# The opening of a two-layer kernel: half means subtracted in one VectorE step, transposes evacuated two blocks at a time, and the second tile centred in halves

## The chip, the cores and the metric

The kernel runs on one core of a Trainium2 chip. The metric is the device time of one execution in microseconds (us).

## The reference

Two layers, each an attention over 8 positions 2 apart and a gated feed-forward part, on 2048 tokens of width 1024. Only the first lines matter here: the layer norm of the input and the projection to q.

```python
def _layernorm(x, axis=-1, eps=1e-5):
    m = jnp.mean(x, axis=axis, keepdims=True)
    v = jnp.var(x, axis=axis, keepdims=True)
    return (x - m) / jnp.sqrt(v + eps)
# ...
x = A_x                                              # [1, 2048, 1024] bf16
x = x + _A_ref(_layernorm(x, axis=-1), A_wqkv, A_wo) # begins with layernorm(x) @ wqkv
```

## The kernel before

The kernel lists its operations with an estimated duration each, places them on a modelled timeline, sorts them by the modelled start and emits them in that order. So a change of one estimate can change the order of instructions on a queue. "AQ" in the model is ScalarE's queue as an issuer of DMAs; the model treats it as an engine beside ScalarE, but line 257 of the kernel issues these DMAs with `nc.scalar.dma_start`, so they stand in one emitted order with ScalarE's own work.

The opening brings 512 tokens (four tiles of 128) and the q weights (eight rows of 256 KB, "row 0" to "row 7") in, and projects the first two tiles while the weights are still landing. The division by the standard deviation is done later, so tiles 0 and 1 need only their mean:

```python
def q_first():
    # x tile 0 in halves on both queues, x tile 1 on ScalarE's; rows 0-4, x tile 3, rows 5, 7 on SyncE's
    # ... cut ...
    dve(0.45, <sum of the left half of x tile 0>,  ..., [("xn", 2), ("part", 0)], -9)
    act(0.75, <sum of the right half of x tile 0>, ..., [("xn", 3), ("part", 1)], -9)
    dma(256, x_sb[2][:], xin[:, 2, :], [("part", 1)], ..., queue="AQ")
    dve(0.16, <mean = (part0 + part1) / D>, ..., [("mean", 0)], -9)
    act(1.15, <mean of x tile 1>, ..., [("xn", 3), ("mean", 1)], -9)
    rows[2](6, queue="AQ", after=[("mean", 1)])       # weight row 6: issued from ScalarE's queue
    for j in range(2):                                # tiles 0 and 1
        # tile 0 centred in halves, tile 1 in one piece (DVE); 8 transposes (PE);
        # first four blocks evacuated by DVE, last four by ACT
        # ... cut ...
    # tiles 2, 3: full layer norm on DVE, then transposes
    # ... cut ...
    for kk, j0, j1 in [(k, j, j + 1) for j in range(2) for k in range(3)] + [(k, 0, 2) for k in range(3, KT)]:
        # 8 (j1 - j0 = 1) or 8 wide matmuls of weight row kk
        # ... cut ...
    wslots[1] = q_weights(1, "s")                     # k weights: two loads of 1 MB, SyncE's queue
```

Of the kernel before, what the change touches and what calls it, by code (L numbers as in the profile page):

```python
# [9 lines left out]
ALU = mybir.AluOpType  # L10
ACTF = mybir.ActivationFunctionType
# [22 lines left out]
class Program:  # L34
# [5 lines left out]
    def add(self, eng, dur, emit, reads=(), writes=(), cls=2, lag=0.0, size=0, takes=(), gives=(), lane=0,  # L40
            table=None):
        op = Op(len(self.ops), eng, dur, emit, tuple(reads), tuple(writes), cls, lag, size, tuple(takes),
                tuple(gives), lane, table)
        for k in op.reads:
            if k in self.last_w:
                op.deps.add(self.last_w[k])
        for k in op.writes:
            if k in self.last_w:
                op.deps.add(self.last_w[k])
            op.deps.update(self.last_r.get(k, ()))  # L50
        op.deps.discard(op)
        for k in op.reads:
            self.last_r.setdefault(k, []).append(op)
        for k in op.writes:
            self.last_w[k] = op
            self.last_r[k] = []
        for a in op.takes + op.gives:
            a.users.append(op)
            a.left += 1
        self.ops.append(op)  # L60
        return op
# [95 lines left out]
def kernel(  # L157
# [11 lines left out]
    nc = tc.nc  # L169
    P = 128  # L170
    _, S, D = A_x.shape
    F = B_w1.shape[1]
    KT = D // P
# [8 lines left out]
    scale = float(Dh) ** -0.5  # L182
# [4 lines left out]
    xin = A_x[0].rearrange("(n p) d -> p n d", p=P)  # L187
# [12 lines left out]
    def alloc(name, shape, dt=BF16):  # L200
        return sb.tile(shape, dt, name=name)

    ident = alloc("ident", [P, P])
# [3 lines left out]
    x_sb = [alloc(f"x{n}", [P, D]) for n in range(S // P)]  # L207
    xnT = [alloc(f"xnT{i}", [P, KT, CH]) for i in range(2)]
    xn = [alloc(f"xn{i}", [P, D]) for i in range(4)]
# [23 lines left out]
    part = alloc("part", [P, 2], FP32)  # L233
    mean = alloc("mean", [P, 2], FP32)
# [5 lines left out]
    pr = Program()  # L240
# [7 lines left out]
    def dve(dur, emit, reads, writes, cls=2, **kw):  # L248
        return pr.add("DVE", dur, emit, reads, writes, cls, **kw)

    def act(dur, emit, reads, writes, cls=0, **kw):
        return pr.add("ACT", dur, emit, reads, writes, cls, **kw)

    def dma(kb, dst, src, reads, writes, cls=3, transpose=False, queue="SP"):
        def emit(op):
            if queue == "AQ":
                nc.scalar.dma_start(dst, src)
            elif transpose:
                nc.sync.dma_start_transpose(dst, src)
            else:  # L260
                nc.sync.dma_start(dst, src)
        return pr.add(queue, 0.45, emit, reads, writes, cls, size=kb * 1024)
# [20 lines left out]
    for i in range(NWARM):  # L283
        a = Acc()
# [66 lines left out]
    def evac(add, dur, emit, last_mm, reads, writes, a, cls=0, **kw):  # L351
        op = add(dur, emit, reads, writes, cls, gives=[a], **kw)
        op.deps.add(last_mm)
        return op
# [62 lines left out]
            q_tile(l, c, which, ws, b)  # L417
        stage_no[0] += 1

    def transposed(src, keys, dst, dkeys):  # L420
        for h, add, fn, dur in ((0, dve, nc.vector.tensor_copy, 0.42), (1, act, nc.scalar.copy, 0.59)):
            a = Acc()
            k0 = 4 * h

            def tr(op, a=a, k0=k0):
                pt = bank[a.bank][:].bitcast(BF16)
                for k in range(4):
                    nc.tensor.transpose(pt[:, k * P:(k + 1) * P], src[:, (k0 + k) * P:(k0 + k + 1) * P], ident[:])  # L428
            tro = pr.add("PE", 0.25, tr, [keys[h], "ident"], [], takes=[a], lag=0.17, lane=2)

            def emit(op, a=a, k0=k0, fn=fn):
                pt = bank[a.bank][:].bitcast(BF16)
                fn(dst[:, k0:k0 + 4, :], pt[:, 0:4 * P].rearrange("p (k t) -> p k t", k=4))  # L433
            evac(add, dur, emit, tro, [], dkeys[k0:k0 + 4], a, cls=-9)

    def q_first():
        for hh in range(2):
            dma(128, x_sb[0][:, hh * 512:(hh + 1) * 512], xin[:, 0, hh * 512:(hh + 1) * 512], [], [("x", 0, hh)], 0,
                queue="AQ" if hh else "SP")
# [3 lines left out]
        for kk in range(5):  # L443
# [3 lines left out]
        rows[2](7)  # L447
        b, q, stats, root, apply = ln(0, first=True)
        ce = hT[:, 8:16, :]
        dve(0.45, lambda _: nc.vector.tensor_scalar(xn[2][:, 0:512], x_sb[0][:, 0:512], 0.0, 0.0, op0=ALU.add,  # L450
                                                    op1=ALU.add, accum_out=part[:, 0:1]),
            [("x", 0, 0)], [("xn", 2), ("part", 0)], -9)
        act(0.75, lambda _: nc.scalar.activation(xn[3][:, 0:512], x_sb[0][:, 512:1024], ACTF.Copy,  # L453
                                                 accum_out=part[:, 1:2]), [("x", 0, 1)], [("xn", 3), ("part", 1)], -9)
        dma(256, x_sb[2][:], xin[:, 2, :], [("part", 1)], [("x", 2, 0), ("x", 2, 1)], 0, queue="AQ")
        dve(0.16, lambda _: nc.vector.tensor_scalar(mean[:, 0:1], part[:, 0:1], part[:, 1:2], 1.0 / D, op0=ALU.add,  # L456
                                                    op1=ALU.mult), [("part", 0), ("part", 1)], [("mean", 0)], -9)
        act(1.15, lambda _: nc.scalar.activation(xn[3][:], x_sb[1][:], ACTF.Copy, scale=1.0 / D,
                                                 accum_out=mean[:, 1:2]), [("x", 1, 0), ("x", 1, 1)],
            [("xn", 3), ("mean", 1)], -9)  # L460
        rows[2](6, queue="AQ", after=[("mean", 1)])
        for j in range(2):
            for h0, h1 in ((0, 1), (1, 2)) if j == 0 else ((0, 2),):
                dve(0.5 if j else 0.32, lambda _, j=j, c0=512 * h0, c1=512 * h1: nc.vector.tensor_scalar(  # L464
                    xn[j][:, c0:c1], x_sb[j][:, c0:c1], mean[:, j:j + 1], None, op0=ALU.subtract),
                    [("x", j, 0), ("x", j, 1), ("mean", j)], [("xn", j)] + [("xn", j, h) for h in range(h0, h1)], -9)
            transposed(xn[j], [("xn", j, h) for h in range(2)], ce[:, :, j * P:(j + 1) * P],
                       [("ce", j, k) for k in range(KT)])
        for j in range(2, TPC):
            stats(j, [("ce", 1, 0)])  # L470
            root(j, j + 1)
            apply(j)
            transposed(xn[j], [("xn", j)] * 2, xnT[b][:, :, j * P:(j + 1) * P],
                       [("xnT", b, j, k // 4) for k in range(KT)])
        for j in range(2):
            act(1.25, lambda _, j=j: nc.scalar.activation(sgt[j][:].rearrange("p a b -> p (a b)"), x_sb[j][:],
                                                          ACTF.Square, bias=mean[:, j:j + 1], scale=-1.0,
                                                          accum_out=part[:, j:j + 1]),
# [3 lines left out]
                                                         scale=1.0 / D),  # L482
# [21 lines left out]
        for kk, j0, j1 in [(k, j, j + 1) for j in range(2) for k in range(3)] + [(k, 0, 2) for k in range(3, KT)]:  # L504
            lk = [q_lhs(wslots[0], kk, m) for m in range(KT)]

            def emit(op, kk=kk, j0=j0, j1=j1, lk=lk, pa=pa):
                for m in range(KT):
                    t0 = (m % 2) * 2 * P
                    nc.tensor.matmul(bank[pa[m // 2].bank][:, t0 + j0 * P:t0 + j1 * P], lhsT=lk[m][0],  # L510
                                     rhs=ce[:, kk, j0 * P:j1 * P], start=(kk == 0 and m % 2 == 0 and j0 == 0),
                                     stop=(kk == KT - 1), skip_group_check=True)
            op = pr.add("PE", 8 * (j1 - j0) * 0.0545, emit,
                        [lk[0][1]] + [("ce", j, kk) for j in range(j0, j1)], [], takes=pa, lag=0.17)
# [193 lines left out]
    def attend(l, c):  # L708
        for r in range(R):
            t_stage(l, c * R + r)  # L710

    q_first()
    attend(0, 0)
    for c in range(1, NCH):
# [47 lines left out]
```

## Time and profile before

| | before |
|---|---|
| time, median of the first 3 runs | 1614.96 us (1614.81 to 1615.19) |
| span of the profiled execution | 1613.4 us |
| TensorE busy | 99% |
| TensorE's gaps after its warm-up | 0.20 us and 0.18 us, both before 6.6 us |
| first full-width projection matmul | 21.89 us |

The page of the kernel before, its line of busy time, and the chain of work that ended last:

```profile
PE 1601.8 (99%) x7463; PEld 763.1 (47%) x7610; DVE 1121.7 (70%) x1904; ACT 330.7 (20%) x527; POOL 5.3 (0%) x28
...
PE 99%; issue 1%; DMA 0%; DVE 0%; ACT 0%
PE bank L347 98%; PE bank L510 0%; PE bank L524 0%; DMA x<-in_A_x_dram 0%; PE bank L428 0%; ACT xn L453 0%; DVE hT L433 0%; DVE xn L464 0%; DVE x L689 0%; DVE mean L456 0%; ACT L281 0%
```

TensorE works without a gap above 0.06 us from 6.52 us to the end.

The timeline of the opening before. Columns: start, length, engine, line, operation, output and input, count, and the idle time of the engine before it with what ended it.

```profile
4.52 0.19 ACT L453 ACTIVATION_READ_ACCUMULATOR xn<-x 128x1 f32 x1
4.74 0.21 DVE L456 TENSOR_SCALAR mean<-part 128x1 f32<-128x1 f32 x1 [0.29 <-ACT xn L453]
4.99 0.62 DVE L464 TENSOR_SCALAR xn<-x,mean 128x512 bf16<-128x512 bf16 x2
...
5.40 0.94 PE L428 MATMUL bank<-ident,xn 128*128 128x128 bf16 x8 [0.20 <-DVE xn L464]
5.42 0.33 ACTq L257 DMA_DIRECT2D slot<-in_A_wqkv_dram  x1
6.04 0.42 DVE L433 COPY hT<-bank 128x512 bf16<-128x512 bf16 x1 [0.44 <-PE bank L428]
...
6.52 1.05 PE L510 MATMUL bank<-hT,slot 128*128 128x128 bf16 x16 [0.18 <-DVE hT L433]
...
7.41 0.61 PE L428 MATMUL bank<-ident,xn 128*128 128x128 bf16 x8
```

Line 456 is the addition that the change removes, line 464 the centring, 428 the transposes, 433 the evacuation, 510 the first weight matmuls. The line at 5.42 is the issue of weight row 6. Later on, the same timeline filtered to TensorE shows an unbroken row of matmuls through row 6's (due at 12.27) and the start of the full-width matmuls:

```profile
10.74 2.56 PE L510 MATMUL bank<-hT,slot 128*128 128x256 bf16 x22
13.14 1.06 PE L428 MATMUL bank<-ident,xn 128*128 128x128 bf16 x16
14.04 1.04 PE L510 MATMUL bank<-hT,slot 128*128 128x256 bf16 x8
...
21.89 2.32 PE L347 MATMUL bank<-xnT,slot 128*128 128x512 bf16 x9
```

### The profile page before, as it was taken

How to read it: one execution, taken by the hardware profiler on the slowest of the kernel's cores; microseconds unless marked ns; L12 is line 12 of the kernel's file. 1: busy time of each engine (PE TensorE's matmuls, PEld its weight loads, DVE VectorE, ACT ScalarE, POOL GpSimd, SP SyncE). 2: the span in 40 equal slices, each digit the busy share in tenths (PEclk: the TensorE clock that was granted, in tenths of full speed). 3: DMA queues.
4: the chain of work that ended last, by engine and by line, in shares of the span. 5: the costliest groups of instructions: out<-in, count | busy, mean ns of one | idle time of the engine just before them, and what ended most of it. 6: DMA issues, size and time to landing. Idle time of an engine off the chain costs nothing.

```text
span 1613.4 us, 19079 instructions
## 1 busy us (share of the span) xinstructions
PE 1601.8 (99%) x7463; PEld 763.1 (47%) x7610; DVE 1121.7 (70%) x1904; ACT 330.7 (20%) x527; POOL 5.3 (0%) x28
## 2 busy tenths in 40 slices
PE   9999999999999999999999999999999999999999
PEld 7555544444444444444444444444444444444444
DVE  5898888889889888888898729884288832211211
ACT  5423322021211222113211032110321101101110
POOL 1000000000000000000000000000000000000000
PEclk9999999999999999999999999999999999999999
DMA  9834755395548664857645487365873464454451
GB/s 318 231 105 150 220 169 171 122 222 167 171 138 251 194 189 134 218 165 227 195 136 162 158 244 231 122 173 178 249 225 119 158 182 156 144 175 152 156 165 44
DMA packets 350649, 285.80 MB, mean 177 GB/s; under 512 B 72288, under 2 KB 344928, under 8 KB 350560
## 3 DMA queue, kind: packets, MB, share of 16 engines
q1 hardware_dynamic: 349984, 283.67, 58.5%
q8 instruction: 59, 0.97, 0.3%
q10 hardware_dynamic: 576, 0.92, 0.2%
q14 instruction: 30, 0.25, 0.1%
HBM read 238.94 MB, written 29.36 MB: 166 GB/s over the span
## 4 chain that ended last, share of the span: by engine, by line
PE 99%; issue 1%; DMA 0%; DVE 0%; ACT 0%
PE bank L347 98%; PE bank L510 0%; PE bank L524 0%; DMA x<-in_A_x_dram 0%; PE bank L428 0%; ACT xn L453 0%; DVE hT L433 0%; DVE xn L464 0%; DVE x L689 0%; DVE mean L456 0%; ACT L281 0%
## 5 line engine op out<-in xcount | busy, mean ns | idle before, releaser
L347 PE MATMUL bank<-xnT,slot 128*128 128x512 bf16 x4955 | 1088.9, 379 | 5.3
L347 PEld LDWEIGHTS <-slot 128*128 128x128 bf16 x5056 | 518.2, 102 | 572.9
L347 PE MATMUL bank<-slot,hT 128*128 128x512 bf16 (+2 forms) x1812 | 387.3, 372 | 1.9
L659 DVE TENSOR_TENSOR hT<-sg,bank 128x512 bf16<-128x512 bf16 x224 | 153.5, 685 | 212.7 <-PE bank L347 196.4
L265 DVE TENSOR_TENSOR scr<-scr 128x1024 bf16<-128x1024 bf16 (+3 forms) x576 | 293.6, 539 | 2.1
L347 PEld LDWEIGHTS <-hT 128*128 128x128 bf16 x1848 | 178.5, 98 | 208.7
L657 ACT ACTIVATE sg<-bank 128x512 bf16<-128x512 f32 x224 | 133.7, 597 | 654.1 <-PE bank L347 613.9
L265 DVE TENSOR_TENSOR scr<-qT,kT 128x2048 bf16<-128x2048 bf16 x128 | 154.2, 1221 | 71.7 <-DMA kT<-qkv_d 70.4
L405 ACT CAST sgt<-bank 128x512 bf16<-128x512 f32 x184 | 107.6, 586 | 288.2 <-PE bank L347 271.3
L265 DVE TENSOR_TENSOR scr<-pA,vT 128x2048 bf16<-128x2048 bf16 x128 | 152.9, 1222 | 0.4
L689 DVE TENSOR_TENSOR x<-x,bank 128x512 bf16<-128x512 bf16 (+1 forms) x66 | 43.7, 671 | 122.6 <-PE bank L347 122.3
L347 PE MATMUL bank<-wo,oT 128*128 128x512 bf16 x502 | 112.6, 379 | 0.5
L313 DVE BATCH_NORM_STATS2 st<-x 128x6 f32<-128x512 bf16 x124 | 81.5, 680 | 12.0 <-DMA x<-in_A_x_dram 11.5
L347 PEld LDWEIGHTS <-oT 128*128 128x128 bf16 x512 | 50.1, 98 | 60.4
L634 DVE TENSOR_TENSOR x<-x,bank 128x512 bf16<-128x512 bf16 x64 | 43.9, 686 | 35.3 <-PE bank L347 33.8
L320 ACT ACTIVATE sd<-mv,epst 128x4 f32<-128x4 f32 (+1 forms) x17 | 5.1, 298 | 183.8 <-DVE mv L316 183.5
L594 DVE STREAM_TRANSPOSE pB<-pA 128x2048 bf16<-128x2048 bf16 x16 | 37.0, 2310 | 0.4
L617 DVE STREAM_TRANSPOSE pA<-pB 128x2048 bf16<-128x2048 bf16 x16 | 36.9, 2309 | 0.4
L657 ACT ACT_TABLE_LOAD x20 | 25.7, 1283 | 51.0 <-PE bank L347 50.8
L265 DVE TENSOR_TENSOR pA<-scr 128x256 bf16<-128x256 bf16 x128 | 35.7, 286 | 0.3
L327 DVE TENSOR_SCALAR xn<-x,mv,rstd 128x1024 bf16<-128x1024 bf16 x62 | 31.0, 542 | 4.9 <-DMA xnT<-xn 4.7
L265 DVE TENSOR_TENSOR oT<-scr 128x256 bf16<-128x256 bf16 x128 | 34.2, 290 | 0.1
(60 smaller groups left out, 211.2 us busy)
## 6 DMA issues: line engine op xcount, KB each, us to landing
slot<-in_B_w_dram SPq DMA_DIRECT2D x160, 1024.0 KB, 5.9
slot<-in_A_wqkv_dram SPq DMA_DIRECT2D x28, 1024.0 KB, 5.3
qkv_d<-sgt SPq DMA_DIRECT2D x92, 256.0 KB, 3.8
qT<-qkv_d SPq DMA_DIRECT2D x16, 512.0 KB, 4.9
slot<-in_B_w_dram SPq DMA_DIRECT2D x16, 512.0 KB, 5.5
kT<-qkv_d SPq DMA_DIRECT2D x14, 544.0 KB, 6.7
vT<-qkv_d SPq DMA_DIRECT2D x14, 544.0 KB, 5.9
out_dram<-x SPq DMA_DIRECT2D x31, 128.0 KB, 4.4
```

The lines of the kernel that those rows point to most:

```text
L265: return lambda _: nc.vector.tensor_tensor(o, a, b, op=op)
L313: dve(0.67, lambda _, hh=hh: nc.vector.bn_stats(st[q][:, j, hh, :], x_sb[n][:, hh * 512:(hh + 1) * 512]), [("x", n, hh)] + list(after), [( ...
L320: act(0.3, lambda _: nc.scalar.activation(sd[q][:, j0:j1], mv[q][:, j0:j1, 1], ACTF.Sqrt, bias=epst[:]), [("mv", q, j) for j in range(j0, ...
L327: dve(0.5, lambda _: nc.vector.tensor_scalar(xn[j][:], x_sb[n][:], mv[q][:, j, 0:1], rstd[q][:, j:j + 1], op0=ALU.subtract, op1=ALU.mult), ...
L347: nc.tensor.matmul(bank[a.bank][:, 0:ncol], lhsT=w, rhs=r, start=first and i == 0, stop=last and i == n - 1)
L405: evac(act, 0.59, lambda _, a=a, i=i, m=m: nc.scalar.copy(sgt[i][:, m % 2, :], bank[a.bank][:]), op, [], [("sgt", i, m % 2)], a)
L594: dve(2.31, lambda _: nc.vector.transpose(psmT[:].rearrange("p c d -> p (c d)"), psm[:].rearrange("p w s -> p (w s)")), allA, ["pB"])
L617: dve(2.31, lambda _: nc.vector.transpose(At[:].rearrange("p w s -> p (w s)"), AeT[:].rearrange("p c d -> p (c d)")), ["pB"], allA)
L634: evac(dve, t1(512), lambda _, xs=xs, a=a: nc.vector.tensor_tensor(xs, xs, bank[a.bank][:], op=ALU.add), op, [("x", n, hh)], [("x", n, hh) ...
L657: evac(act, 0.6, lambda _, i=i, a=ag: nc.scalar.activation(sg[i][:], bank[a.bank][:], ACTF.Silu), og, [], [("sg", i)], ag, table="silu")
L659: evac(dve, t1(512), lambda _, i=i, a=au, f=f: nc.vector.tensor_tensor(hT[:, f, :], sg[i][:], bank[a.bank][:], op=ALU.mult), ou, [("sg", i ...
L689: evac(dve, t1(cn), lambda _, xs=xs, a=a, cn=cn: nc.vector.tensor_tensor(xs, xs, bank[a.bank][:, 0:cn], op=ALU.add), op, [("x", n, hh)], [ ...
```

## The change

The intent: tile 0 reaches the first weight matmul sooner. The two half means are no longer added; the centring subtracts both, as two scalars of one instruction. The first evacuation waits for two transposes instead of four. Tile 1 is centred in halves, so that its first transposes start before the second half is done. The diff, cut to its core:

```diff
-    def transposed(src, keys, dst, dkeys):
-        for h, add, fn, dur in ((0, dve, nc.vector.tensor_copy, 0.42), (1, act, nc.scalar.copy, 0.59)):
+    def transposed(src, keys, dst, dkeys, pieces=((0, 4, "DVE"), (4, 8, "ACT"))):
+        for k0, k1, eng in pieces:
+            n = k1 - k0
+            add, fn, dur = ((dve, nc.vector.tensor_copy, 0.15 + n * 0.0675) if eng == "DVE" else
+                            (act, nc.scalar.copy, 0.2 + n * 0.0975))
# ... n transposes and one evacuation of n blocks each ...
-        dve(0.45, lambda _: nc.vector.tensor_scalar(xn[2][:, 0:512], x_sb[0][:, 0:512], 0.0, 0.0, op0=ALU.add,
-                                                    op1=ALU.add, accum_out=part[:, 0:1]),
+        dve(0.77, lambda _: nc.vector.tensor_scalar(xn[2][:, 0:512], x_sb[0][:, 0:512], 1.0 / D, 0.0, op0=ALU.mult,
+                                                    op1=ALU.add, accum_out=mean[:, 0:1]),
-        act(0.75, ... ACTF.Copy, accum_out=part[:, 1:2]) ...
+        act(0.82, ... ACTF.Copy, scale=1.0 / D, accum_out=part[:, 0:1]) ...
-        dve(0.16, lambda _: nc.vector.tensor_scalar(mean[:, 0:1], part[:, 0:1], part[:, 1:2], 1.0 / D, op0=ALU.add,
-                                                    op1=ALU.mult), ...
-        act(1.15, ... mean of x tile 1 ...
+        act(1.25, ... mean of x tile 1 ...
         rows[2](6, queue="AQ", after=[("mean", 1)])
+                    dve(0.31, lambda _, c0=c0: nc.vector.tensor_scalar(
+                        xn[0][:, c0:c0 + 512], x_sb[0][:, c0:c0 + 512], mean[:, 0:1], part[:, 0:1], op0=ALU.subtract,
+                        op1=ALU.subtract), ...                       # tile 0, in halves
+                    dve(0.31, ... xn[1] half, mean[:, 1:2], None, op0=ALU.subtract ...)   # tile 1, in halves
+                       ((0, 2, "DVE"), (2, 4, "DVE"), (4, 8, "ACT")) if j == 0 else ((0, 4, "DVE"), (4, 8, "ACT")))
+        dve(0.16, ... mean[:, 0:1] += part[:, 0:1], after tile 1's evacuation (needed for the variance) ...)
```

More of the change, by code (lines that the diff above doesn't have):

```diff
@@ L418, in q_stage, with tr, emit @@
         stage_no[0] += 1
-    def transposed(src, keys, dst, dkeys):
-        for h, add, fn, dur in ((0, dve, nc.vector.tensor_copy, 0.42), (1, act, nc.scalar.copy, 0.59)):
+    def transposed(src, keys, dst, dkeys, pieces=((0, 4, "DVE"), (4, 8, "ACT"))):
[3 more added lines that the diff above has]
+                            (act, nc.scalar.copy, 0.2 + n * 0.0975))
             a = Acc()
-            k0 = 4 * h
-            def tr(op, a=a, k0=k0):
+            def tr(op, a=a, k0=k0, n=n):
                 pt = bank[a.bank][:].bitcast(BF16)
-                for k in range(4):
+                for k in range(n):
                     nc.tensor.transpose(pt[:, k * P:(k + 1) * P], src[:, (k0 + k) * P:(k0 + k + 1) * P], ident[:])
-            tro = pr.add("PE", 0.25, tr, [keys[h], "ident"], [], takes=[a], lag=0.17, lane=2)
-            def emit(op, a=a, k0=k0, fn=fn):
+            tro = pr.add("PE", 0.0625 * n, tr, [keys[k0 // 4], "ident"], [], takes=[a], lag=0.17, lane=2)
+            def emit(op, a=a, k0=k0, k1=k1, n=n, fn=fn):
                 pt = bank[a.bank][:].bitcast(BF16)
-                fn(dst[:, k0:k0 + 4, :], pt[:, 0:4 * P].rearrange("p (k t) -> p k t", k=4))
-            evac(add, dur, emit, tro, [], dkeys[k0:k0 + 4], a, cls=-9)
+                fn(dst[:, k0:k1, :], pt[:, 0:n * P].rearrange("p (k t) -> p k t", k=n))
+            evac(add, dur, emit, tro, [], dkeys[k0:k1], a, cls=-9)
     def q_first():
@@ L449, in q_first @@
         ce = hT[:, 8:16, :]
-        dve(0.45, lambda _: nc.vector.tensor_scalar(xn[2][:, 0:512], x_sb[0][:, 0:512], 0.0, 0.0, op0=ALU.add,
-                                                    op1=ALU.add, accum_out=part[:, 0:1]),
-            [("x", 0, 0)], [("xn", 2), ("part", 0)], -9)
-        act(0.75, lambda _: nc.scalar.activation(xn[3][:, 0:512], x_sb[0][:, 512:1024], ACTF.Copy,
-                                                 accum_out=part[:, 1:2]), [("x", 0, 1)], [("xn", 3), ("part", 1)], -9)
-        dma(256, x_sb[2][:], xin[:, 2, :], [("part", 1)], [("x", 2, 0), ("x", 2, 1)], 0, queue="AQ")
-        dve(0.16, lambda _: nc.vector.tensor_scalar(mean[:, 0:1], part[:, 0:1], part[:, 1:2], 1.0 / D, op0=ALU.add,
-                                                    op1=ALU.mult), [("part", 0), ("part", 1)], [("mean", 0)], -9)
-        act(1.15, lambda _: nc.scalar.activation(xn[3][:], x_sb[1][:], ACTF.Copy, scale=1.0 / D,
+        dve(0.77, lambda _: nc.vector.tensor_scalar(xn[2][:, 0:512], x_sb[0][:, 0:512], 1.0 / D, 0.0, op0=ALU.mult,
+                                                    op1=ALU.add, accum_out=mean[:, 0:1]),
+            [("x", 0, 0)], [("xn", 2), ("mean", 0)], -9)
+        act(0.82, lambda _: nc.scalar.activation(xn[3][:, 0:512], x_sb[0][:, 512:1024], ACTF.Copy, scale=1.0 / D,
+                                                 accum_out=part[:, 0:1]), [("x", 0, 1)], [("xn", 3), ("part", 0)], -9)
+        dma(256, x_sb[2][:], xin[:, 2, :], [("part", 0)], [("x", 2, 0), ("x", 2, 1)], 0, queue="AQ")
+        act(1.25, lambda _: nc.scalar.activation(xn[3][:], x_sb[1][:], ACTF.Copy, scale=1.0 / D,
                                                  accum_out=mean[:, 1:2]), [("x", 1, 0), ("x", 1, 1)],
@@ L462, in q_first @@
         for j in range(2):
-            for h0, h1 in ((0, 1), (1, 2)) if j == 0 else ((0, 2),):
-                dve(0.5 if j else 0.32, lambda _, j=j, c0=512 * h0, c1=512 * h1: nc.vector.tensor_scalar(
-                    xn[j][:, c0:c1], x_sb[j][:, c0:c1], mean[:, j:j + 1], None, op0=ALU.subtract),
-                    [("x", j, 0), ("x", j, 1), ("mean", j)], [("xn", j)] + [("xn", j, h) for h in range(h0, h1)], -9)
+            for h in range(2):
+                c0 = 512 * h
+                if j == 0:
+                    dve(0.31, lambda _, c0=c0: nc.vector.tensor_scalar(
+                        xn[0][:, c0:c0 + 512], x_sb[0][:, c0:c0 + 512], mean[:, 0:1], part[:, 0:1], op0=ALU.subtract,
+                        op1=ALU.subtract), [("x", 0, 0), ("x", 0, 1), ("mean", 0), ("part", 0)],
+                        [("xn", 0), ("xn", 0, h)], -9)
+                else:
+                    dve(0.31, lambda _, c0=c0: nc.vector.tensor_scalar(
+                        xn[1][:, c0:c0 + 512], x_sb[1][:, c0:c0 + 512], mean[:, 1:2], None, op0=ALU.subtract),
+                        [("x", 1, 0), ("x", 1, 1), ("mean", 1)], [("xn", 1), ("xn", 1, h)], -9)
             transposed(xn[j], [("xn", j, h) for h in range(2)], ce[:, :, j * P:(j + 1) * P],
-                       [("ce", j, k) for k in range(KT)])
+                       [("ce", j, k) for k in range(KT)],
+                       ((0, 2, "DVE"), (2, 4, "DVE"), (4, 8, "ACT")) if j == 0 else ((0, 4, "DVE"), (4, 8, "ACT")))
+        dve(0.16, lambda _: nc.vector.tensor_tensor(mean[:, 0:1], mean[:, 0:1], part[:, 0:1], op=ALU.add),
+            [("mean", 0), ("part", 0), ("ce", 1, 0)], [("mean", 0)], -9)
         for j in range(2, TPC):
```

## The prediction

> What bounds it now. The page gives TensorE 99% of a 1613.4 us span at full granted clock; the chain of work that ended last is 98% the projection matmuls (line 347). The timeline's TensorE gaps are all before 6.6 us: 0.20 us before tile 0's transposes, 0.18 us before the first weight matmul. From 6.52 us on TensorE never waits, so only time saved in the opening, and kept until TensorE runs unbroken (about 15 us), shortens the span.
>
> What changes, from the timeline of the first 15 us:
> 1. The addition of the two half sums goes (0.21 us, 4.74 to 4.95, plus dispatch; centring started at 4.99). The centring with two scalars can start when ScalarE's accumulator read ends (4.71), at 4.74: 0.25 us earlier. I estimate the same length for it: with two scalars 1024 columns take 0.49 us back to back in line 327, with one 0.48.
> 2. The first VectorE eviction waits for two transposes instead of four. TensorE is still at half clock there: transposes start 0.106 us apart, against 0.056 us later, which is what the Trainium skill ("TensorE: Matmul & The Clock Gate", section "Wait — 56ns, not 53.3ns?") gives for cold and warm. That is worth 0.21 us. The eviction itself shrinks from 0.425 to an estimated 0.29 us (a fixed 0.16 plus half the rest): 0.13 us.
> So the first weight matmul could start near 5.92; TensorE is itself busy with eight cold transposes until about 5.97, so I expect 5.97 instead of 6.52: 0.55 us.
> 3. The rest of tile 1 doesn't move as much: its mean comes from ScalarE at 6.53, fixed by the landing of x tile 1 (5.29). Centred in halves, its first half ends near 6.9 (before: 7.05 for all). TensorE arrives at about 6.91 and waits to 6.95. Gain there: 0.40 us.
> 4. Weights: landings I read for rows 2, 3, 4, 5 are 7.03, 7.79, 8.63, 11.16. Row 5 was needed at about 11.40. With a 0.4 us gain TensorE asks at about 11.0, and waits 0.1 to 0.2 us. This takes half of the gain back.
> 5. The instruction order shows that the issue of weight row 6 on ScalarE's queue moves behind the tile 0 eviction and waits for row 2: about 7.05 instead of 5.42. It landed at 10.98 behind x tile 2 in that queue (9.13); I expect 11 to 11.6; needed at about 12.1: no wait, and rows and x tile 3 on the other queue may come a little earlier.
> 6. One more reciprocal ahead of each apply of tiles 2 and 3 delays these by about 0.07 us (12.55 to 12.62, 13.20 to 13.28). TensorE needs them at about 12.9 and 13.35: barely on time.
>
> Sum: 0.55 us at the first matmul, 0.40 after tile 1's transposes, about 0.2 us after row 5. From there it is carried to the end unchanged: the TensorE order is otherwise the same, with banks renamed by one.
>
> Predicted 1614.75 us, a gain of 0.21 us or 0.013%; range 1614.2 to 1615.3, mostly the spread of runs (1614.81 to 1615.19). Chances: faster by over 2% 0.00, within 2% 0.99, slower 0.01.
>
> In the profile: tile 0's centring at 4.74; first weight matmul at 5.9 to 6.0; no gap or a short one before tile 1's transposes; a gap of 0.1 to 0.2 us before row 5's matmuls, put down to the weight load; row 6's issue near 7.05; the first full-width projection matmul (line 347) 0.15 to 0.3 us earlier than 21.89.
>
> What would make it wrong: the clock's rise from half to full (about 6.1 us here) falling elsewhere; row 6 landing after 12.1; x tile 3 or row 5 landing at other times; the two-scalar centring running slower.

## The result

| | before | changed |
|---|---|---|
| time, median of 6 runs | 1615.01 us (1614.81 to 1615.19) | 1615.48 us (1614.85 to 1616.04) |
| ratio, with its 95% interval | | 1.0003 (0.999 to 1.0016) |
| span of the profiled execution | 1613.4 us | 1614.1 us |
| first weight matmul | 6.52 us | 5.73 us |
| start of row 6's matmuls | 12.27 us | 13.02 us |
| first full-width matmul | 21.89 us | 22.66 us |

A ratio is the mean time of one kernel's fast runs over that of the other's fast runs of the same rounds, so it is not quite the ratio of the medians in the table. The two kernels are the same within 2%; the interval holds 1. The median lies 0.18 us above the predicted range.

The six single times tell more than the median: 1614.85, 1615.04, 1615.04 and 1615.92, 1616.02, 1616.04. There is no run within 0.4 us of the median. The changed kernel has two kinds of executions about 1 us apart; the kernel before has one (all 42 of its runs lie between 1614.71 and 1615.56). The profiled execution is of the upper kind (1615.92), so the profile shows the loss.

The timeline of the opening of the changed kernel (line 466 is the centring with two scalars, 430 the transposes, 435 the evacuation, 471 tile 1's centring, 520 the weight matmuls):

```profile
4.20 0.19 ACT L455 ACTIVATION_READ_ACCUMULATOR xn<-x 128x1 f32 x1
4.42 0.73 DVE L466 TENSOR_SCALAR xn<-x,mean,part 128x512 bf16<-128x512 bf16 x2 [0.24 <-ACT xn L455]
...
4.99 0.69 PE L430 MATMUL bank<-ident,xn 128*128 128x128 bf16 x8
5.38 0.49 DVE L435 COPY hT<-bank 128x256 bf16<-128x256 bf16 x2 [0.23 <-PE bank L430]
...
5.73 1.05 PE L520 MATMUL bank<-hT,slot 128*128 128x128 bf16 x16
...
6.39 0.62 DVE L471 TENSOR_SCALAR xn<-x,mean 128x512 bf16<-128x512 bf16 x2 [0.52 <-ACT xn L458]
6.76 0.34 ACTq L257 DMA_DIRECT2D slot<-in_A_wqkv_dram  x1
...
6.80 0.66 PE L430 MATMUL bank<-ident,xn 128*128 128x128 bf16 x8
```

The opening does what it should: the first weight matmul comes 0.79 us earlier, tile 1's transposes 0.61 us earlier (part of this is luck of the execution: x tile 0's second half landed at 3.64 instead of 3.96, x tile 1 at 5.12 instead of 5.29). But row 6 is issued at 6.76 instead of 5.42. TensorE's timeline further on:

```profile
10.83 1.04 PE L520 MATMUL bank<-hT,slot 128*128 128x256 bf16 x8
13.02 1.05 PE L520 MATMUL bank<-hT,slot 128*128 128x256 bf16 x8 [1.16 <-DMA slot<-in_A_wqkv_dram]
13.91 1.06 PE L430 MATMUL bank<-ident,xn 128*128 128x128 bf16 x16
...
22.66 1.67 PE L347 MATMUL bank<-xnT,slot 128*128 128x512 bf16 x6
```

The matmuls at 13.02 are row 6's. The matmul before them started at 11.59, and these start 0.109 us apart, so they were due at 11.70, 0.57 us earlier than before (12.27), and started 1.32 us late. (The profile's gap of 1.16 us is shorter, as it counts from the modelled end of the matmul before, not from when the next was due.) 0.57 - 1.32 = -0.75, and the first full-width matmul is 0.77 us later than before. From there on nothing differs: from the first full-width matmul to the end of the span the traces have 1591.46 to 1591.48 us in every profiled run of this document except e7 (1591.88). So a run's time is set by its opening. The chain of the first 25 us, followed back, in order of time (start, length, what), names the cause by the time of the issue and of the landing:

```profile
6.36 0.40 ACT hT L435
6.76 6.22 DMA slot<-in_A_wqkv_dram
12.98 0.05 issue
13.02 1.05 PE bank L520 x8
```

What moved row 6's issue? In the kernel's own model, tile 0's ScalarE evacuation now starts at 5.09 and row 6's issue at 5.19; before these were 5.23 and 5.09. So the emitted order on ScalarE's queue flipped. With it the completion semaphores of the DMAs (the listing of the instruction order and the traces name eight, used again and again) went to other loads. In that listing, row 6 now waits until row 2's load has freed its semaphore, and the first load of k weights, which had this wait before, waits for x tile 1's instead. In the trace: row 2 landed at 6.74, row 6 was issued at 6.76; the k load, which before was issued at 7.05, was issued at 6.66, a tenth of a microsecond ahead of row 6.

### The profile page after: what moved, and what is told of

Its sections match the earlier page's. It is cut to its first block, busy times and chain, and to the rows that moved or that the text cites. A ratio compares the mean times of both kernels' runs of the same rounds, so it can differ in the third digit from the quotient of the medians.

```text
span 1614.1 us, 19082 instructions
## 1 busy us (share of the span) xinstructions
PE 1601.8 (99%) x7463; PEld 762.8 (47%) x7610; DVE 1122.1 (70%) x1906; ACT 331.1 (21%) x527; POOL 5.3 (0%) x28
## 4 chain that ended last, share of the span: by engine, by line
PE 99%; DMA 1%; issue 0%; ACT 0%; DVE 0%; ACTq 0%
PE bank L347 98%; PE bank L534 0%; DMA slot<-in_A_wqkv_dram 0%; DMA x<-in_A_x_dram 0%; PE bank L520 0%; ACT xn L458 0%; PE bank L430 0%; ACT L281 0%; ACT hT L435 0%; DVE x L699 0%; ACTq L458 0%
## 5 line engine op out<-in xcount | busy, mean ns | idle before, releaser
L313 DVE BATCH_NORM_STATS2 st<-x 128x6 f32<-128x512 bf16 x124 | 81.6, 680 | 12.1 <-DMA x<-in_A_x_dram 11.7
```

Of the source, the lines that this page charges most:

```text
L313: dve(0.67, lambda _, hh=hh: nc.vector.bn_stats(st[q][:, j, hh, :], x_sb[n][:, hh * 512:(hh + 1) * 512]), [("x", n, hh)] + list(after), [( ...
```

## The experiments

Theory A: row 6 lands late because it is issued next to and mostly behind the first 1 MB load of k weights; which of the two goes first is a race of about 0.1 us, and this makes the two kinds of executions. Rival B: the two kinds come from TensorE's clock, whose rise from half to full falls at different times. Rival C: all loads are late in the slow kind. Later a rival of A was added: the late issue alone makes row 6 late, whatever is beside it.

Landings below are read from the trace as the arrival of the sixteenth part of a load at its semaphore. All experiments gave correct results. The times of each run are beside 9 runs of the kernel before on the same chip: medians 1614.98 (first four runs), 1614.94 (e4 to e7), 1614.92 (e8 and the three looks), 1615.07 (e9, e10). All ratios of timed runs against before lie within 0.9997 and 1.0004 with intervals of about 0.13% to each side, except e8; so what follows rests on the groups of times and on the traces, not on these ratios.

### after_again: the changed kernel, once more

> The changed kernel itself, once more, for a second profile and more times. Theory A (weight row 6 is issued close behind the first 1 MB load of k weights and lands after a part of it; which of the two is issued first is a race of about 0.1 us): times in two groups again, near 1615.0 and near 1616.0, and in the profile the gap before row 6's matmuls goes with the group: about 1.2 us at 1616, about 0.2 us or none at 1615. Rival B (the clock's rise from half to full falls at different times): the two groups go with the time of the rise, and the gap before row 6's matmuls is the same in both.

No edit. Measured: 1615.86, 1615.70, 1615.13, 1614.82, 1616.28: two groups again. The profiled one (1615.86) has row 6 issued at 6.97, after the k load (6.59), landed at 12.93, and a gap of 1.13 us.

### e1_row6_early: row 6's issue put back

```diff
+        for op, ref, dt in getattr(self, "moved", ()):      # in the placement, before the sort
+            op.start = ref.start + dt
         placed.sort(key=lambda o: (o.start, o.seq))
         rows[2](6, queue="AQ", after=[("mean", 1)])
+        pr.moved = [(pr.ops[-1], pr.ops[-2], 0.001)]        # row 6 right behind tile 1's mean
```

> The change, with the issue of weight row 6 put back ahead of tile 0's ScalarE eviction, nothing else changed. Theory A: issued near 5.3 us, landed by 11.2, no gap of TensorE above 0.3 us after 6.9 us, one group of times, 1614.3 to 1614.8, 0.2 to 0.6 us below before in the same rounds. Rival B: two groups about 1 us apart remain. Rival C (row 6 lands late because all loads are late in such executions): the gap before row 6 remains about 1 us.

Measured: 1614.69 to 1615.07, median 1614.79, one group; before 1614.98. Row 6 issued at 5.24, landed at 10.72. TensorE's timeline has one gap above 0.1 us after the first weight matmul, before tile 1's transposes:

```profile
6.79 0.66 PE L432 MATMUL bank<-ident,xn 128*128 128x128 bf16 x8 [0.34 <-DVE xn L474]
7.28 4.90 PE L523 MATMUL bank<-hT,slot 128*128 128x128 bf16 x57
```

The gap is the wait for tile 1's mean, ahead of the 6.9 us from which I had expected none; the times reach a little above the range that I had expected. The loss and the second group are gone. So the place of row 6's issue, with the hand-out of semaphores that follows from it (the k load waits for row 2 again, and is issued at 6.97), is the cause of both; the arithmetic part of the change, without it, is about 0.2 us below before by the medians. Rival B has nothing to stand on here, as nothing was done to the clock; it falls for good with after_third and after_fourth below, where TensorE is at full pace from 4.9 us in both and the times are of different groups. Rival C falls too: in the slow profile of the changed kernel rows 5 and 7 landed a microsecond earlier than before (10.12 and 10.80, against 11.16 and 11.82); only row 6 was late.

### e2_k_held: row 6 left where the change put it, the k loads held back

```diff
+        for i in (2, 3):
+            pr.add("POOL", 0.1, lambda _, i=i: nc.gpsimd.tensor_copy(slot[i][:, 0:1], hT[:, 12, 0:1]), [("ce", 0, 4)],
+                   [("w", i, k) for k in range(4)])
         wslots[1] = q_weights(1, "s")
```

> The change, with row 6 still issued behind tile 0's ScalarE eviction, but the two 1 MB loads of k weights held back until that eviction has ended (a one-column copy on GpSimd into each slot). Theory A: row 6 is issued near 6.3, ahead of the k weights (about 7.1), and lands by 11.6: no gap or under 0.2 us before its matmuls, times 1614.3 to 1614.9 in one group. A rival of A (the later issue alone makes row 6 late, whatever is issued next to it): it lands after 12.1 and the gap stays above 0.3 us. The k weights land about 0.5 us later than 15.6, needed only after 21 us: no cost.

Measured: 1614.79 to 1615.13, median 1615.02, one group; three of its five runs lie above the expected 1614.9. Row 6 landed at 10.81, and there was no gap before its matmuls. But the semaphores were handed out differently again: row 6 got one that was already free and was issued at 5.54, not near 6.3. So this run doesn't separate a late issue from a bad neighbour. It does show that standing behind the evacuation in the queue costs nothing: the evacuation itself started only at 6.45. What had delayed row 6 was the wait for row 2's semaphore.

### e3_before_row6_late: the kernel before, with only the order of the change

```diff
+        row6 = pr.ops[-1]                                   # in the kernel before
+        pr.moved = [(row6, <tile 0's ScalarE evacuation>, 0.001)]
```

> The kernel before, with only the order part of the change: row 6 issued behind tile 0's ScalarE eviction. Theory A: issue near 7.05 (it waits for row 2), next to the first load of k weights at about 6.97; landing near 13; row 6's matmuls, due at 12.27, wait 0.7 to 0.9 us; time 0.5 to 0.9 us over before. Rivals B and C: no difference from before, within 0.2 us.

Measured: 1614.92, 1614.94, 1615.02 and 1615.88, 1616.25. The kernel before, which never showed it, now has the two groups. I had expected all runs to be slow; it is a race here too. Its profile fell in the lower group (1614.94): row 6 was issued at 6.69, as late as in the changed kernel, but 0.14 us before the k load (6.84), and landed at 11.65, in time. That is the first sign that the neighbour counts, not the lateness.

### e4_row7_first and e4_again: row 7 used before row 6

```diff
-[(k, 0, 2) for k in range(3, KT)]
+[(k, 0, 2) for k in (3, 4, 5, 7, 6)]
# ... and row 6, now the last, ends the accumulation: stop=(kk == 6) ...
```

> The change with nothing moved on any queue, but TensorE uses weight row 7 before row 6, so that row 6 is needed after both pairs of transposes, near 13.6 us, instead of 11.9. Theory A: row 6 may still land at 11.6 or at 12.9, as the race goes, but no gap follows; one group of times, 1614.4 to 1615.1. If the loss came from anything else than waiting for row 6, two groups 1 us apart remain.

> Row 7 before row 6 once more. Theory A: if row 6 is issued after the first load of k weights here, it lands near 12.95 and yet no gap above 0.1 us follows; time 1614.5 to 1614.9 either way.

Measured, five timed runs: 1614.53 to 1614.80, median 1614.77, no gap at all in the profile (row 6 landed at 11.48). The further look: 1615.67, with row 6 issued at 7.06, after the k load (6.58), landed at 14.51, and a gap of 0.77 us where I had expected none. So this order lowers the loss and doesn't remove it: row 6 can land later than the 13.8 us at which it was then needed.

### e5_centring_only and e6_pieces_only: the two parts alone

```diff
# e5: e1, and
-((0, 2, "DVE"), (2, 4, "DVE"), (4, 8, "ACT")) if j == 0 else ((0, 4, "DVE"), (4, 8, "ACT")))
+((0, 4, "DVE"), (4, 8, "ACT")))
# e6: the kernel before with the new transposed(), row 6 early, and
+((0, 2, "DVE"), (2, 4, "DVE"), (4, 8, "ACT")) if j == 0 else ((0, 4, "DVE"), (4, 8, "ACT")))
```

> The change with row 6 put back ahead, and tile 0 evicted four blocks at a time as before: two-scalar centring and tile 1 in halves remain. Theory A, with tile 1's mean as the limit: first weight matmul about 0.25 us later than with both parts (about 1.4 us after the end of ScalarE's accumulator read of tile 0, against 1.17), but tile 1's transposes at the same 1.65 to 1.7 us after the landing of x tile 1, so the same time as with both parts within 0.1 us: 1614.6 to 1615.0. Rival: the two-block eviction carries through, and the time is 0.2 us or more above that of e1_row6_early.

> The kernel before with only the two-block eviction of tile 0, row 6's issue as before. Tile 1 is centred in one piece, so its transposes come about 1.8 to 2.0 us after the landing of x tile 1, whatever tile 0 gains. Time between that of e1_row6_early and that of before, 1614.8 to 1615.1; a gap of 0.4 us or more before tile 1's transposes. Rival: the gain at the first weight matmul is kept, and the time is that of e1_row6_early or less.

Measured: e5 1614.94 to 1615.81, median 1615.16, outside what I expected (its run at 1615.81 lies among the upper group's times although row 6 is issued early in this kernel; its only profile is of the run at 1614.94, so this stays unexplained); e6 1614.84 to 1615.12, median 1614.94, as expected in its time but with a gap before tile 1's transposes of only about 0.1 us instead of 0.4, and 0.34 us before row 5, which landed late in its profile (11.32). In e5 the first four transposes of tile 1 start at 6.75, as close to the landing of x tile 1 (5.07) as expected, but the kernel's model had moved them ahead of row 1's eight matmuls, so that TensorE was about 0.4 us behind e1 at row 3 (its matmuls at 9.44 instead of 9.07). As row 5 was in time here and late in e1, 0.14 us of this was left at the first full-width matmul (21.68 and 21.54). So e5 doesn't measure the two-block evacuation alone. The split of the gain between the parts stays open: neither part alone was shown to gain anything over before.

### e7_x1_first: x tile 1 ahead of the weights

```diff
-        dma(256, x_sb[1][:], xin[:, 1, :], [], [("x", 1, 0), ("x", 1, 1)], 0, queue="AQ")
+        for hh in range(2):
+            dma(128, <half hh of x tile 1>, [], [("x", 1, hh)], 0, queue="AQ" if hh else "SP")
```

> As e1_row6_early, but x tile 1 is loaded in two halves ahead of all weight rows. If the landing of x tile 1 bounds tile 1's transposes, the gap of 0.34 us before them goes away and they start 0.2 to 0.4 us earlier; but the loads as a whole bound what follows: row 5 lands no earlier than 10.9, and the gap before its matmuls grows from 0.05 to 0.2 to 0.4 us. Time within 0.15 us of e1_row6_early. Rival (the opening is bound by engines, not by loads): the time falls by 0.2 us or more.

Measured: 1615.30 to 1616.03, median 1615.40, 0.6 us more than e1, where I had expected the same time. The gap before tile 1's transposes went away, as expected, and gaps opened later: 0.29 us before row 5 (landed at 11.08), and 0.14 us before tile 2's transposes, because x tiles 2 and 3 landed at 9.91 and 10.40 instead of 8.96 and 9.76. The opening is bound by its loads: what is loaded sooner makes something else later. About 0.4 us of its profiled time was lost after the first full-width matmul and was not followed up. This profile, with no idle time before row 6's matmuls, is of a run at 1616.03: a time near 1616 alone doesn't show that row 6 was late.

### e8_row6_behind: row 6 always behind the k load

```diff
+        pr.moved = [(row6, <tile 1's ScalarE evacuation>, 0.001)]
```

> The change with row 6 issued behind tile 1's ScalarE eviction, so certainly after the first load of k weights (about 6.6). Theory A: issued at 7.4 to 7.9, landing at 13 or later in every execution, gap of 1.1 us or more before its matmuls; one group of times, 1615.8 to 1617.5, none near 1615.0. If the group was chosen by something else than the order of the two issues (clock's rise, launch), two groups remain.

Measured: 1619.43 to 1621.15, median 1620.93, ratio 1.0034. None is near 1615, as expected, but all are 1.9 to 3.7 us above my range, and they are not clearly one group: four lie from 1620.64 to 1621.15, one 1.2 us below them. Row 6, issued at 7.71, came after both loads of k weights (7.02 and 7.51). It landed at 15.55, with the first of them (15.73), and TensorE waited 3.87 us:

```profile
15.60 0.82 PE L524 MATMUL bank<-hT,slot 128*128 128x256 bf16 x3 [3.87 <-DMA slot<-in_A_wqkv_dram]
```

The table of stretches of this run (start and end, length, busy time and count of TensorE, weight loads, VectorE, ScalarE and GpSimd, granted clock, DMA share, GB/s) shows what that cost in addition:

```profile
12.00:15.50 3.50, 0.00 (x0) 0.00 (x0) 1.58 (x5) 0.38 (x2) 2.38 (x12) 0.83 1.05 394
15.50:21.00 5.50, 5.40 (x34) 4.28 (x35) 1.30 (x3) 2.36 (x5) 0.83 (x5) 0.50 0.74 111
```

The clock is at half until 21 us: 0.50 in the third column from the right. By an estimate 5.5 us at half clock lose 2.7 us; with the gap of 3.87 that is 6.6, less about 0.5 us that the opening had gained: 6.1, against 6.0 us measured between the spans (1619.4 and 1613.4).

### after_third and after_fourth: two more looks at the changed kernel

> The changed kernel, one more look. Theory A: if row 6 is issued before the first load of k weights, it lands by 11.7, no gap above 0.1 us before its matmuls, and the time is 1614.8 to 1615.2; if after, it lands near 12.95, the gap is 1.1 us and the time 1615.7 to 1616.3.

> The same as for after_third: the order of the two issues decides the landing of row 6, the gap and the time.

Measured: after_third 1615.12: row 6 issued at 6.863, the k load at 6.873; landed at 12.16; gap 0.09 us. So the lower group does have the lower gap; it landed 0.5 us later than I had said. after_fourth 1616.11: row 6 issued at 7.34, the k load at 7.52, so row 6 was first, and yet it landed at 13.19 with a gap of 1.06 us. This is against the simple form of theory A. Of the sixteen parts of row 6 eleven had landed by 12.13 and five came at 12.81 to 13.19; row 7, issued at 7.05 on the other queue, was spread in the same way (10.31 to 12.99). In this execution row 1 landed late (6.66, against 5.79 in the first profile), which cost TensorE a gap of 0.56 us before row 1's matmuls and pushed the issues of rows 5, 7 and 6 close to the k load's.

### e10_late_alone: late, but with no k load beside it

```diff
# e8, and
+        for i in (2, 3):
+            pr.add("POOL", 0.1, lambda _, i=i: nc.gpsimd.tensor_copy(slot[i][:, 0:1], hT[:, 12, P:P + 1]), [("ce", 1, 4)],
+                   [("w", i, k) for k in range(4)])
```

> Row 6 issued as late as in e8_row6_behind or a little earlier (7.0 to 7.8), but both loads of k weights held until tile 1's ScalarE eviction has ended (about 8.2 or later), so that row 6 is late without a neighbour. Theory A (the neighbour makes it late): row 6 lands by 11.9, gap 0.3 us or less, times 1614.6 to 1615.3 in one group. Rival (a late issue alone makes it late): it lands at 12.5 or later, a gap of 0.6 us or more, times 1615.5 or more.

Measured: 1614.66 to 1614.98, median 1614.71, one group; before 1615.07. Row 6 was issued later than in any other run, at 7.84, with the k load at 8.78:

```profile
7.84 0.34 ACTq L259 DMA_DIRECT2D slot<-in_A_wqkv_dram  x1
```

The issues of that moment, with the median time from issue to landing in the last column:

```profile
slot<-in_A_wqkv_dram ACTq DMA_DIRECT2D x1, 256.0 KB, 4.1
```

And the same for the changed kernel, where the k load is in the same tenth of a microsecond:

```profile
slot<-in_A_wqkv_dram SPq DMA_DIRECT2D x1, 1024.0 KB, 8.9
slot<-in_A_wqkv_dram ACTq DMA_DIRECT2D x1, 256.0 KB, 6.2
```

And for e8, where the 1 MB load in the same window is the second one of k weights:

```profile
slot<-in_A_wqkv_dram SPq DMA_DIRECT2D x1, 1024.0 KB, 10.9
slot<-in_A_wqkv_dram ACTq DMA_DIRECT2D x1, 256.0 KB, 7.8
```

4.1 us without the neighbour, 6.2 us and 7.8 us with it. Some of this is only the later issue, as the loads ahead had got further; row 7's landing is a fairer mark: row 6 landed 0.66 us after it here (11.29 and 11.95), and 2.18 us after it in the changed kernel (10.80 and 12.98). Row 6 landed 0.05 us later than I had said, and no gap followed. The late issue alone is harmless; the k load beside it does the harm. This settles the rival of A.

The packets show how. ScalarE's DMAs are q10 of the traces (0.92 MB in the whole run, the size of ScalarE's four loads), SyncE's are q1. The view of the DMA queues, cut to a stretch of time, gives what each moved: in the changed kernel row 6's 0.26 MB took from 10.0 to 12.5 us, in which q1 moved 0.71 MB; after row 7 had landed only k weights were left on q1, and 0.63 MB of them went by from 10.80 to 12.98. In e10 the 0.26 MB were through between 10.0 and 11.5, and in e3 between 9.5 and 11.0, each beside 0.32 MB on q1. So in the changed kernel the packets of row 6 and of the k load went through the DMA engines in the same stretch of time, and row 6 took the longer for it.

### e9_early_6_before_5: the candidate for the best version

```diff
# e1, and
-[(k, 0, 2) for k in range(3, KT)]
+[(k, 0, 2) for k in (3, 4, 6, 5, 7)]
```

> Row 6 issued early as in e1_row6_early, and used before row 5, in the order in which the two landed there (10.72 and 10.98), with the gap of 0.045 us before row 5. Candidate for the best version. Theory A: no gap after tile 1's transposes, one group of times, 1614.6 to 1615.0, at or up to 0.1 us below e1_row6_early (1614.69 to 1615.07 there).

Measured: 1614.77 to 1614.99, median 1614.95, before 1615.07; no gap after tile 1's transposes, one group. It is no better than e1. In its profile TensorE ran at half clock until about 6.3 us (weight matmuls 0.107 us apart, then 0.056), later than in any other look, and its first weight matmul came at 5.95 against 5.39 in e1.

### All looks in one table

Times in us. "Gap" is TensorE's idle time before row 6's matmuls by the profile, "time" that of the profiled execution. In e4 and e4_again row 7 is used before row 6, in e9 row 6 before row 5.

| kernel | row 6 issued | k load issued | row 6 landed | gap | time |
|---|---|---|---|---|---|
| before | 5.42 | 7.05 | 10.98 | none | 1615.14 |
| e1 | 5.24 | 6.97 | 10.72 | none | 1614.79 |
| e2 | 5.54 | 7.38 | 10.81 | none | 1614.82 |
| e10 | 7.84 | 8.78 | 11.95 | none | 1614.98 |
| e5 | 5.20 | 6.77 | 10.39 | none | 1614.94 |
| e6 | 5.18 | 7.29 | 11.07 | none | 1615.12 |
| e7 | 5.99 | 6.75 | 12.16 | none | 1616.03 |
| e9 | 5.36 | 6.83 | 10.80 | none | 1614.77 |
| e3 | 6.69 | 6.84 | 11.65 | none | 1614.94 |
| e4 | 6.44 | 6.59 | 11.48 | none | 1614.53 |
| after_third | 6.86 | 6.87 | 12.16 | 0.09 | 1615.12 |
| after_fourth | 7.34 | 7.52 | 13.19 | 1.06 | 1616.11 |
| after | 6.76 | 6.66 | 12.98 | 1.16 | 1615.92 |
| after_again | 6.97 | 6.59 | 12.93 | 1.13 | 1615.86 |
| e4_again | 7.06 | 6.58 | 14.51 | 0.77 | 1615.67 |
| e8 | 7.71 | 7.02 | 15.55 | 3.87 | 1621.15 |

Wherever the k load was issued first, row 6 landed at 12.9 or later. Wherever row 6 was first, it landed by 12.2, with one exception (after_fourth).

## Why the prediction was wrong

The step that failed is point 5: "I expect 11 to 11.6; needed at about 12.1: no wait". I had seen that row 6's issue moves to about 7.05 and waits for row 2; it moved to 6.76, and row 2 had landed at 6.74. What I got wrong is the landing: 12.98 in the profiled execution, needed at 11.70, so that TensorE started 1.32 us late (1.16 us of it idle by the profile). I reasoned that row 6 stands behind x tile 2 in its own queue and starts when that ends. I looked only at its own queue. The other queue had the k load, which lost its wait in the same reshuffle and was issued at about the same moment; experiments e1, e3, e8 and e10 together show that this neighbour makes the difference, and the packets that the two shared the DMA engines. The listing that I had before me showed both halves, and I drew no conclusion from the second.

The other points:

- Point 1: the two-scalar centring did start right after the accumulator read, 0.035 us after it. It takes longer than I said: in the trace 0.41 us for 512 columns against 0.35 with one scalar, and the second starts 0.33 us after the first instead of 0.27. I had compared back-to-back starts of line 327 with the length of one instruction of line 464. In this execution the term cost nothing: the first half was centred at 4.83, and the first transpose started at 4.99, right behind TensorE's last warm-up matmul (4.56, 0.43 us long).
- Point 2: right in kind. The first weight matmul came at 5.73, not 5.97: x tile 0 was 0.32 us early in this execution, and TensorE was at full clock from 5.2 us and not from 6.1; that part is luck. The two-block evictions took 0.29 and 0.28 us, as estimated.
- Point 3: tile 1's transposes at 6.80, predicted 6.95; its mean is their limit, as said (the wait is on line 471).
- Point 4: there was no wait for row 5. It landed at 10.12, a microsecond earlier than before: with row 6 out of the way, the rows behind it moved up. In e1, where row 6 is ahead of row 5 again, row 5 landed at 10.98 and TensorE waited for it: 0.045 us idle by the profile, but the matmul started 0.318 us after the one before instead of 0.109, so 0.21 us late, at the upper end of the 0.1 to 0.2 us predicted. So this term was sound where row 6 is in time.
- Point 6: the applies of tiles 2 and 3 ended at 12.20 and 12.86, earlier than before despite the extra reciprocals, because x tile 3 landed at 9.45 instead of 10.31. Neither cost anything.
- The gain after tile 1's transposes was predicted as 0.40 us; it was 0.57 us at row 3's matmuls (9.08 instead of 9.65) and when row 6's weights were missing. 0.17 us of it is as much as x tile 1 landed earlier in this execution (5.12 and 5.29), which is luck. About 0.2 us is left of the gain in e1 against before, by medians. One pair of profiles can't show a gain of that size: e3, with the arithmetic of the kernel before, has its first full-width matmul at 21.67, 0.22 us earlier than before's.
- The range: it was taken from the spread of the kernel before. The changed kernel has a race that the kernel before doesn't have, and its 13 executions divide into six from 1614.82 to 1615.13 and seven from 1615.70 to 1616.28. A median of such a set can fall into the hole between the groups.

The prediction named "row 6 landing after 12.1" as something that would make it wrong. It did.

What stays open: why row 6 was late in after_fourth although it was issued first (a spread of the sixteen parts of both rows 6 and 7 was seen, its cause not); how the gain divides between centring and evacuation; and what sets the moment of the clock's rise.

Versions e1 and e10 have a lower median than both kernels (1614.79 and 1614.71, against 1614.98 and 1615.07 of before in their calls) and one group of times. The difference from before, 0.2 to 0.4 us in 1615, is below what the intervals of the ratios resolve.

## What to carry to other kernels

When an order of emission decides which DMA gets which semaphore, a change of one engine's work can move waits between loads that have nothing to do with it: compare the waits of every DMA in the old and the new order, and for a load that moved, ask which loads of the other queues are now issued beside it. A load that is needed soon should not be issued in a race with a large one that is needed late; hold the large one back with a true dependency, or issue the small one well ahead. And look at the single times before the median: two groups are a race, and a profile shows only one of them.

## What the Trainium skill lacked or had wrong

- "DMA: Bandwidth & Descriptors", section "Queues, rings and completion order", says that each DMA engine takes turns between the queues that have work, packet by packet. The changed kernel's profile agrees where row 6 met the k load (0.20 MB of q10 beside 0.63 MB of q1 from 10.80 to 12.98 us). What the page lacks is when a load's turn begins: rows 5, 7 and 6 were issued at 5.81, 6.18 and 6.76, with the k load at 6.66, and landed at 10.12, 10.80 and 12.98; from 8.5 to 10.0 us q1 moved 0.60 MB and q10 nothing, although row 6 had been issued and x tile 2 ahead of it on its queue had landed at 8.78. Up to there the loads came in the order of issue over both queues; why is not shown. The section "Issuing engines are not separate DMA queues" of the same page says that DMAs of all issuers interleave; the page lacks that 0.1 us in the order of two issues can go with 0.8 us in the landing of a 256 KB load (12.16 in after_third, where row 6 was issued 0.01 us ahead of the k load; 12.98 in the first profile of the same kernel, where it was 0.10 us behind).
- "TensorE: Matmul & The Clock Gate", section "Part 1: The HAM clock gate", says that the rise to full clock varies by about 0.5 us to each side. The first instructions at full pace lie between about 3.6 us (e7) and 6.4 us (e9) here, with the same warm-up matmuls from 0.77 us on. Its statement that an idle window of about 3.4 us brings the clock back to half agrees with e8 in kind: half clock after a gap of 3.87 us. But the granted 0.83 between 12.00 and 15.50 us puts the drop, by an estimate, at about 14.3 us, 2.6 us into that gap.
- "DVE: scalar operands, raw-bit mode, write accounting and state across instructions", section "Scalar operands", gives no cost of a second per-partition scalar: 0.41 us against 0.35 us for 512 bf16 columns here.
